# A softmax-convolution and cosine-FFN kernel: every product in two halves of 64 rows

## The chip, the core and the metric

The kernel runs on one core of a Trainium2 chip. The metric is the device time of one execution in microseconds (us). The engines are named as in the profile: PE (TensorE matmuls), PEld (TensorE weight loads), DVE (VectorE), ACT (ScalarE), POOL (GpSimd) and SP (SyncE, which issues the DMAs).

## The reference

Inputs are `x` (8 x 4096 x 192), `weight_gen` (8 x 4096 x 8 x 7), `w_in` (192 x 2048) and `w_out` (2048 x 192); the first two are float32, the weights float64.

```python
w = softmax(weight_gen, axis=-1)                        # 7 taps for each of 8 heads
a[b, s, h, :] = sum_k w[b, s, h, k] * x_padded[b, s + k, h, :]   # causal, 24 channels a head
h = a.reshape(32768, 192) @ w_in                        # 32768 x 2048
out = (h * cos(h)) @ w_out                              # 32768 x 192
```

## The kernel before, in words

**Tiling.** The 32768 tokens lie over 128 partitions, 256 in a row on each. A block is 4 tokens of every partition, 512 in all, and there are 64 blocks. POOL mixes the taps of a block into `xa` (lines 225 to 245). For each of the 4 tokens PE transposes `xa` in two pieces (line 257), channels 0 to 127 and the last 64 channels twice, so that both reach 128 rows. ACT and DVE split the transposed rows, divided by 2 pi, into two float32r parts whose sum is nearly exact: `a_hi`, `a_lo` for 128 channels and `b_hi`, `b_lo` for the 64 doubled ones (lines 264 and 265).

**First product** (line 282). A pair is two chunks of 128 of the 2048 columns of `w_in`; a block has 8 pairs and the program 512. A pair writes one tile `h` of 128 x 1024 (two PSUM banks) from a ring of three. Each chunk takes 5 matmuls of 512 columns: three for the 128 channels (low x high, high x low, high x high), two for the 64 channels, where `wb` holds the high part of the weights in rows 0 to 63 and the low part in rows 64 to 127 and the rows of `b` are there twice.

**Elementwise work** of pair i, on the 128 x 1024 of `h`: ACT rounds to `turn` (line 292), DVE subtracts (296), ACT takes the sine (300), DVE multiplies into `h` (303), ACT makes the high part `ghi` (309), DVE the low part `glo` in bf16 (313). Lines 309 and 313 are issued one pair later. The tile `h` is free after line 313.

**Second product.** A half of a block's chunks (8) is contracted at once for each token: 8 matmuls of 384 columns with `ghi` as weights (line 329) and 8 of 192 columns with `glo` (line 332), into a tile `ps_m` of one bank out of two. ACT copies it out (335) and POOL adds the two halves of the block and the two parts of the columns (346, 347). This follows the first product by 6 pairs (`LAG`), one group of 16 matmuls for each pair.

**Order.** Each engine issues in the order of the program, which is written out by the main loop: for pair i the first product, at pairs 5 and 6 of a block one of the two transposes (four matmuls) of the next block, the elementwise work of i, and then the second product of i - 6. The softmax of 16 rows (4 blocks) is done a step a pair, in 15 batches inside the loop: DVE maximum (179), POOL difference (181), ACT exponential (184), DVE sum (188, 189) and reciprocal (191), POOL product (193). The exponential and the next sine each load a table on ACT. While the first blocks run, the float64 words of the weights are converted on ACT, DVE and POOL (lines 112 to 132).

Of the kernel before, what the change touches and what calls it, by code (L numbers as in the profile page):

```python
# [20 lines left out]
P = 128  # L21
# [10 lines left out]
# sin(SIN_SCALE * f + SIN_BIAS) = cos(2 pi f) for -3/4 <= f <= 1/4; both constants are a few ulp  # L32
# below 2 pi and pi / 2, so that the argument stays within the table's [-pi, pi].
# [3 lines left out]
# The upper word of 2.0 ** -127 in float64, read as a float32: smaller values become denormal.  # L37
# [4 lines left out]
def tile_softmax_conv_then_cos_ffn(  # L42
# [58 lines left out]
    def two_parts(raw, hi, lo, half=None):  # L101
# [19 lines left out]
        # sign, exponent and 20 bits of the mantissa  # L121
# [3 lines left out]
        # 3 more bits of the mantissa  # L125
# [12 lines left out]

    def w_in_b(j):
        raw = words(CW)  # L140
        cols = [slice(n * (F // 2) + j * CW, n * (F // 2) + (j + 1) * CW) for n in range(2)]
        for n in range(2):
            nc.sync.dma_start(out=raw[n * D2:(n + 1) * D2], in_=w_in[P:D, cols[n]].bitcast(I32))

        def convert():
            parts = gpool.tile([P, 2, CW], F32R, name="parts", tag="ghi")
            yield from two_parts(raw, parts[:, 0, :], parts[:, 1, :])
            for n in range(2):
                for m in range(2):
# [64 lines left out]
    def attention(b, eng, ra=0, rb=R, spare=False):  # L214
# [3 lines left out]
        # the columns from D on repeat the last D2, for both halves of the transposed rows  # L218
# [14 lines left out]
        for k in range(1, K + 1):  # L233
            if k < K:
                if spare:
                    pr = work.tile([P, R, D], F32, name="pr", tag="turn", bufs=TMP)
                else:
                    pr = work.tile([P, R, D], F32, name="pr", bufs=3)
                product(k, pr[:, ra:rb])
                yield  # L240
# [10 lines left out]
    xT = {}  # L251

    def transposed(b, part):
        xa = mixed[b]
        tr = ps_m.tile([P, CT], F32, name="ps_m")
        for r in range(R):
            nc.tensor.transpose(  # L257
                tr[:, r * P:(r + 1) * P], xa[:, r, (0, P)[part]:(P, P + 2 * D2)[part]], ident)
        hi = work.tile([P, CT], F32R, name="ab"[part] + "_hi")
        lo = work.tile([P, CT], F32R, name="ab"[part] + "_lo")  # L260
        xT.setdefault(b, []).extend((hi, lo))

        def split():
            nc.scalar.activation(out=hi, in_=tr, func=AF.Copy, scale=1.0 / TWO_PI)
            nc.vector.scalar_tensor_tensor(  # L265
                out=lo, in0=tr, scalar=1.0 / TWO_PI, in1=hi.bitcast(F32),
                op0=ALU.mult, op1=ALU.subtract)

        return split

# [1 line left out]
    hs, g_parts = {}, {}  # L272

    def ffn_in(i):
        b, pair = divmod(i, NPAIR)
        a_hi, a_lo, b_hi, b_lo = xT[b]
        h = ps_h.tile([P, 2, CT], F32, name="h")
        for n in range(2):
            fs = slice((2 * pair + n) * P, (2 * pair + n + 1) * P)
            prods = ((wa_hi, a_lo), (wa_lo, a_hi), (wb, b_lo), (wb, b_hi), (wa_hi, a_hi))  # L280
            for m, (w, v) in enumerate(prods):
                nc.tensor.matmul(h[:, n, :], lhsT=w[:, fs], rhs=v,  # L282
                                 start=(m == 0), stop=(m == len(prods) - 1))
        hs[i] = h

# [30 lines left out]
    sums, finals = {}, {}  # L316

    def ffn_out(j):
        b, m = divmod(j, 2 * R)
        half, t = divmod(m, R)  # L320
        acc = ps_m.tile([P, CT], F32, name="ps_m")
        ts = slice(t * P, (t + 1) * P)
        for m in range(2):
            for c in range(2 * HALF):
                pair, n = divmod(c, 2)
                g = g_parts[b * NPAIR + half * HALF + pair][m][:, n, ts]
                fc = half * 2 * HALF + c
                if m == 0:
                    nc.tensor.matmul(acc[:, 0:2 * D], lhsT=g, rhs=wo[:, fc, :],  # L329
                                     start=(c == 0), stop=False)  # L330
                else:
                    nc.tensor.matmul(acc[:, 0:D], lhsT=g, rhs=wo_b[:, fc, :],  # L332
                                     start=False, stop=(c == 2 * HALF - 1))
        part = work.tile([P, 2 * D], F32, name=f"part{half}", bufs=(5 if half == 0 else 2))
        nc.scalar.activation(out=part, in_=acc[:, 0:2 * D], func=AF.Copy, scale=TWO_PI)  # L335
        if half == 0:
            sums[(b, t)] = part
            return
        if t == 0:
# [3 lines left out]
        old = sums.pop((b, t))  # L343
        last = b == NB - 1
        eng = nc.vector if last else nc.gpsimd
        eng.tensor_tensor(out=part, in0=part, in1=old, op=ALU.add)  # L346
        eng.tensor_tensor(out=fin[:, t, :], in0=part[:, 0:D], in1=part[:, D:2 * D], op=ALU.add)
        if t == R - 1 or (last and t == R - 2):
            t0 = t if last and t == R - 1 else 0
# [73 lines left out]
    for split in splits:  # L423
        split()
# [89 lines left out]
```

## Time and profile before

| | |
|---|---|
| runs | 2419.05 us median of 3 (2418.82 to 2419.44) |
| profiled execution: span from first to last instruction | 2416.5 us |
| PE busy | 2345.7 us |
| PEld busy | 2019.7 us |
| DVE busy | 2037.1 us |
| ACT busy | 1848.9 us |
| POOL busy | 1877.6 us |
| mean granted TensorE clock | 0.992 |

The profiled execution is one run of the program; its span is 2.55 us under the median of the runs. Matmuls are pipelined: the time that one takes in the rows (about 0.4 us) holds its way through the array, and what it costs in a stream is the distance between the starts of two. A weight load has a row of its own on PEld and lies beside the matmul before it.

### The profile page before, as it was taken

To read this page: it belongs to the slowest core of one execution; us is meant where nothing else is said; L and a number is where in the kernel's file an instruction comes from. 1 tells how busy PE (TensorE), PEld (TensorE's weight loads), DVE (VectorE), ACT (ScalarE), POOL (GpSimd) and SP (SyncE) were. 2 spreads that over 40 slices of the span, in tenths; PEclk is the share of its full clock that TensorE was granted. 3 is DMA by queue.
4 is the path that set the end of the run, shared out by engine and by line. 5 is a ranking of instruction groups with operands and counts; after the bars stand their busy time and mean duration, and the time that the engine had idled before them with its cause. 6 is when DMAs were issued, how large, how long until landed. Compare 5 with 4: busy or idle time off the path is not lost.

```text
span 2416.5 us, 34582 instructions
## 1 busy us (share of the span) xinstructions
PE 2345.7 (97%) x13824; PEld 2019.7 (84%) x13824; DVE 2037.1 (84%) x1820; ACT 1848.9 (77%) x2266; POOL 1877.6 (78%) x1458
## 2 busy tenths in 40 slices
PE   2799999999999999999999999999999999999999
PEld 1588888888888888888888888888888888888888
DVE  8988888888888888888888888888888888888887
ACT  3678777787877778777787777878777787777876
POOL 6698878797787787787787787877877877887841
PEclk8899999999999999999999999999999999999999
DMA  6211220210211120121211211111111201201100
GB/s 163 53 42 36 47 54 24 54 47 23 54 47 31 46 54 24 47 51 27 54 37 33 54 35 43 47 27 51 46 31 47 54 24 46 54 24 48 30 7 20
DMA packets 25456, 104.93 MB, mean 43 GB/s; under 512 B 2782, under 2 KB 5462, under 8 KB 25294
## 3 DMA queue, kind: packets, MB, share of 16 engines
q1 hardware_dynamic: 25294, 102.72, 17.1%
q8 instruction: 108, 1.77, 0.3%
q14 instruction: 54, 0.44, 0.1%
HBM read 76.50 MB, written 25.17 MB: 42 GB/s over the span
## 4 chain that ended last, share of the span: by engine, by line
PE 87%; DVE 6%; ACT 5%; issue 1%; DMA 0%; SPq 0%; ACTq 0%; DVEq 0%
PE h L282 46%; PE ps_m L329 27%; PE ps_m L332 13%; PE ps_m L257 2%; ACT ghi L309 1%; ACT turn L292 1%; DVE h L303 1%; DVE glo L313 1%; DVE den L189 1%; ACT L300 1%; DVE turn L296 1%; ACT turn L300 1%; DVE t L114 1%; ACT L184 1%; DVE den L188 1%
## 5 line engine op out<-in xcount | busy, mean ns | idle before, releaser
L296 DVE TENSOR_TENSOR turn<-h,turn 128x1024 f32<-128x1024 f32 x512 | 625.5, 1222 | 326.3 <-ACT turn L292 323.3
L329 PE MATMUL ps_m<-wo,ghi 128*128 128x384 f32 x4096 | 812.9, 340 | 3.1 <-ACT part L335 3.1
L292 ACT ACTIVATE turn<-h 128x1024 int32<-128x1024 f32 x512 | 524.7, 1025 | 314.3 <-PE h L282 314.3
L329 PEld LDWEIGHTS ps_m<-wo,ghi 128*128 128x128 f32 x4096 | 721.1, 188 | 38.3 <-ACT part L335 3.6
L245 POOL TENSOR_TENSOR xa<-xa,pr 128x768 f32<-128x768 f32 (+1 forms) x384 | 705.4, 1837 | 5.0
L300 ACT ACTIVATE turn<-turn 128x1024 f32<-128x1024 f32 x512 | 543.4, 1061 | 184.2 <-DVE turn L296 184.0
L303 DVE TENSOR_TENSOR h<-h,turn 128x1024 f32<-128x1024 f32 x512 | 629.9, 1230 | 8.3 <-ACT turn L300 8.3
L313 DVE TENSOR_TENSOR glo<-h,ghi 128x1024 bf16<-128x1024 f32 x512 | 621.7, 1214 | 1.1 <-ACT ghi L309 1.1
L225 POOL TENSOR_TENSOR pr<-xt,taps 128x768 f32<-128x768 f32 (+1 forms) x384 | 588.2, 1537 | 0.0
L346 POOL TENSOR_TENSOR part<-part,part 128x384 f32<-128x384 f32 x252 | 256.3, 1017 | 391.2 <-ACT part L335 391.1
L309 ACT CAST ghi<-h 128x1024 fp32r<-128x1024 f32 x512 | 516.3, 1008 | 3.8 <-DVE h L303 2.8
L282 PE MATMUL h<-a_lo,wa_hi 128*128 128x512 f32 x1024 | 454.3, 444 | 33.2 <-DVE glo L313 25.5
L332 PE MATMUL ps_m<-wo_b,glo 128*128 128x192 bf16 x4096 | 426.8, 247 | 0.0
L282 PE MATMUL h<-a_hi,wa_hi 128*128 128x512 f32 x1024 | 408.0, 398 | 0.0
L282 PE MATMUL h<-a_hi,wa_lo 128*128 128x512 f32 x1024 | 406.8, 397 | 1.1 <-POOL wa_lo L132 1.1
L282 PE MATMUL h<-b_hi,wb 128*128 128x512 f32 x1024 | 404.6, 395 | 0.0
L282 PE MATMUL h<-b_lo,wb 128*128 128x512 f32 x1024 | 403.6, 394 | 0.8 <-DVE b_lo L265 0.8
L332 PEld LDWEIGHTS <-glo 128*128 128x128 bf16 x4096 | 311.7, 98 | 82.1 <-issue 82.1
L282 PEld LDWEIGHTS h<-a_lo,wa_hi 128*128 128x128 f32 x1024 | 194.7, 190 | 62.6 <-ACT wa_hi L128 13.6
L335 ACT ACTIVATE part<-ps_m 128x384 f32<-128x384 f32 x512 | 241.4, 472 | 6.8 <-PE ps_m L332 6.8
L282 PEld LDWEIGHTS h<-b_lo,wb 128*128 128x128 f32 x1024 | 194.2, 190 | 48.9 <-DVE b_lo L265 1.3
L282 PEld LDWEIGHTS h<-b_hi,wb 128*128 128x128 f32 x1024 | 194.2, 190 | 45.5
(52 smaller groups left out, 1285.6 us busy)
## 6 DMA issues: line engine op xcount, KB each, us to landing
xt<-in_x_dram SPq DMA_DIRECT2D x62, 960.0 KB, 7.4
out_dram<-fin SPq DMA_DIRECT2D x63, 384.0 KB, 3.9
taps<-in_weight_gen_dram SPq DMA_DIRECT2D x15, 448.0 KB, 8.6
raw<-in_moe_w_out_dram SPq DMA_DIRECT2D x8, 384.0 KB, 3.9
raw<-in_moe_w_in_dram SPq DMA_DIRECT2D x6, 256.0 KB, 6.6
raw<-in_moe_w_in_dram SPq DMA_DIRECT2D x3, 512.0 KB, 5.9
wb<-parts SPq DMA_DIRECT2D x8, 128.0 KB, 4.8
xt<-in_x_dram SPq DMA_DIRECT2D x1, 768.0 KB, 11.7
```

The costliest lines, as they stand in the source:

```text
L225: eng.tensor_tensor(out=dst.rearrange("p r (h g) -> p r h g", h=H), in0=xt[:, k + ra:k + rb, :].rearrange("p r (h g) -> p r h g", h=H), in ...
L245: eng.tensor_tensor(out=xa[:, ra:rb, 0:D], in0=xa[:, ra:rb, 0:D], in1=old[:, ra:rb], op=ALU.add)
L282: nc.tensor.matmul(h[:, n, :], lhsT=w[:, fs], rhs=v, start=(m == 0), stop=(m == len(prods) - 1))
L292: nc.scalar.activation(out=t.bitcast(I32), in_=hs[i], func=AF.Identity, bias=0.25, scale=1.0)
L296: nc.vector.tensor_tensor(out=t, in0=hs[i], in1=t.bitcast(I32), op=ALU.subtract)
L300: nc.scalar.activation(out=t, in_=t, func=AF.Sin, bias=SIN_BIAS, scale=SIN_SCALE)
L303: nc.vector.tensor_tensor(out=hs[i], in0=hs[i], in1=turns.pop(i), op=ALU.mult)
L309: nc.scalar.copy(out=hi, in_=hs[i])
L313: nc.vector.tensor_tensor(out=lo, in0=hs.pop(i), in1=hi.bitcast(F32), op=ALU.subtract)
L329: nc.tensor.matmul(acc[:, 0:2 * D], lhsT=g, rhs=wo[:, fc, :], start=(c == 0), stop=False)
L332: nc.tensor.matmul(acc[:, 0:D], lhsT=g, rhs=wo_b[:, fc, :], start=False, stop=(c == 2 * HALF - 1))
L346: eng.tensor_tensor(out=part, in0=part, in1=old, op=ALU.add)
```

## The change

**Halves.** The array is used as two tiles of 64 rows, rows 0 to 63 and rows 64 to 127, which take their weights and their moving data from the same partitions. A product over 128 rows becomes two matmuls, one for each half, written one behind the other in the program. The two write different PSUM banks at one time. Since both halves of a sum belong in the same bank, they trade: in a first part the lower half writes bank 0 and the upper half bank 1, in a second part it is the other way round. Between the parts stands `traded`, a no-operation on SP that reads the tile: PE starts the second part when SP has passed, and SP passes when the first part has landed.

**First product.** A pair has 3 matmuls of each half in the first part (`ffn_in_first`) and 6 in the second (`ffn_in_second`). The 64 channels take 3 products over 64 rows (low x high, high x low, high x high): the two halves hold them for the two chunks. `wb` becomes `wb_hi` and `wb_lo`, loaded with the chunks of odd number in the upper rows, without the copies by DMA. The 6 pairs before the second product begins use whole products for the 128 channels and halves for the 64 (`ffn_in_whole`).

**Second product.** A group is two tokens and one half of the chunks. It takes two pairs (s = 0 and 1), each with 16 matmuls of 384 and 16 of 192 columns over 64 rows, into a tile `acc` of two banks, of which there is one. One ACT copy of 128 x 768 takes it out after the second pair, and POOL adds on 768 columns. The last 6 pairs use whole products.

**Order in the loop.** A pair i issues on PE the first part of h(i), the second product of i - 6, and the second part of h(i). The elementwise work of pair i comes in the next turn of the loop.

**Transposes.** For blocks 7 to 63 the transposes are four matmuls of 64 columns for each token, two in each pair, written to columns 384 to 511 of the two banks of `acc` between the `ghi` and the `glo` matmuls. ACT and DVE split them (`x_hi`, `x_lo`, 128 x 2 x 128) behind the copy of `acc`. Blocks 1 to 6 (`WHOLE`) are transposed whole, at pair 5, into a tile of the ring `h`.

**The rest.** The store of a block is issued three pairs later, the rows of the next block are loaded in the middle of a block's mixing, and `pr` has two buffers where it had three.

```diff
-    ps_m = ctx.enter_context(tc.tile_pool(name="ps_m", bufs=2, space=bass.MemoryType.PSUM))
+    ps_m = ctx.enter_context(tc.tile_pool(name="ps_m", bufs=1, space=bass.MemoryType.PSUM))
...
+    def traded(t):
+        nc.sync.keepalive_nop([nc.sync.lower_ap(t)])
...
+    def split(b, tr, cs):
+        hi, lo = parts_of(b)
+        nc.scalar.activation(out=hi[:, :, cs], in_=tr, func=AF.Copy, scale=1.0 / TWO_PI)
+        yield
+        nc.vector.scalar_tensor_tensor(
+            out=lo[:, :, cs], in0=tr, scalar=1.0 / TWO_PI, in1=hi[:, :, cs].bitcast(F32),
+            op0=ALU.mult, op1=ALU.subtract)
...
+    def transpose_all(b):
+        xa = mixed[b]
+        tr = ps_h.tile([P, 2, CT], F32, name="h")
...
+    def transpose_row(b, r, acc, s):
+        xa = mixed[b]
+        for q in range(2):
+            rs = slice(q * D2, (q + 1) * D2)
+            nc.tensor.matmul(acc[:, q ^ s, 2 * D + q * D2:2 * D + (q + 1) * D2],
+                             lhsT=xa[rs, r, columns(q ^ s)], rhs=ident[rs, rs], is_transpose=True,
...
+    def ffn_in_first(i):
+        h = ps_h.tile([P, 2, CT], F32, name="h")
+        for m, (w, v) in enumerate(((wa_hi, x_lo), (wa_lo, x_hi), (wa_hi, x_hi))):
+            for q in range(2):
+                rs = slice(q * D2, (q + 1) * D2)
+                nc.tensor.matmul(
+                    h[:, q, :], lhsT=w[rs, chunk(pair, q)], rhs=v[rs, 0, :],
...
+        traded(h)
...
+    def ffn_in_second(i):
+        prods = ((wa_hi, x_lo, 0), (wa_lo, x_hi, 0), (wb_hi, x_lo, 1), (wb_lo, x_hi, 1),
+                 (wa_hi, x_hi, 0), (wb_hi, x_hi, 1))
+        for m, (w, v, part) in enumerate(prods):
+            for q in range(2):
+                cs = chunk(pair, 1 - q) if part == 0 else slice(pair * P, (pair + 1) * P)
+                nc.tensor.matmul(
+                    h[:, 1 - q, :], lhsT=w[rs, cs], rhs=v[rs, part, :],
...
     def ffn_out(j):
+        if s == 0:
+            accs[group] = ps_m.tile([P, 2, CT], F32, name="acc")
...
+                for q in range(1 if whole else 2):
+                    rs = slice(0, P) if whole else slice(q * D2, (q + 1) * D2)
+                    bank = q ^ s
+                    t = 2 * tp + bank
+                    to, w = (acc[:, bank, 0:2 * D], wo) if lo == 0 else (acc[:, bank, 0:D], wo_b)
+                    nc.tensor.matmul(
+                        to, lhsT=g[rs, n, t * P:(t + 1) * P], rhs=w[rs, fc, :],
...
+            if lo == 0:
+                bt = group // R + 2
+                if WHOLE < bt < NB:
+                    transpose_row(bt, group % R, acc, s)
+        if s == 0 and not whole:
+            traded(acc)
...
+    def evacuate(j):
+        nc.scalar.activation(out=part, in_=acc[:, :, 0:2 * D], func=AF.Copy, scale=TWO_PI)
+        if WHOLE < bt < NB:
+            yield from split(bt, acc[:, :, 2 * D:], slice(r * P, (r + 1) * P))
...
-    for i in range(N + LAG):
+    for i in range(N + LAG + 1):
+        if 0 <= i - 1 < N:
+            act_turns(i - 1)
+        if 0 <= i - 2 < N:
+            act_hi(i - 2)
...
+            dve_fraction(i - 1)
+            act_cos(i - 1)
...
+            dve_lo(i - 2)
...
+            dve_g(i - 1)
...
+            if i < N:
+                ffn_in_first(i)
+            ffn_out(j)
+            if i < N:
+                ffn_in_second(i)
+        if pair == TR and b + 1 <= WHOLE:
+            until_mixed(b + 1)
+            tr = (transpose_all(b + 1),)
...
+            all_of(evacuate(j), *tr)
```

How the order moves on PE is shown for one pair in the middle of the program, from the first product of a pair to the first `glo` product. Before, the second chunk of a pair (`h`) is followed by the group of the second product (`ps_m`):

```order
L282 MATMUL h<-a_lo,wa_hi 128x512
L282 MATMUL h<-a_hi,wa_lo 128x512
L282 MATMUL h<-b_lo,wb 128x512
L282 MATMUL h<-b_hi,wb 128x512
L282 MATMUL h<-a_hi,wa_hi 128x512
L329 MATMUL ps_m<-wo,ghi 128x384 x8
L332 LDWEIGHTS glo
L332 MATMUL ps_m<-wo_b,glo 128x192
```

After the change the same engine issues the second part of one pair (line 343), the first part of the next (326), the `ghi` products (400) and two transposes (290); "x2" and "x16" are the two halves in turn:

```order
L343 MATMUL h<-x_lo,wa_hi 128x512 x2
L343 MATMUL h<-x_hi,wa_lo 128x512 x2
L343 MATMUL h<-x_lo,wb_hi 128x512 x2
L343 MATMUL h<-x_hi,wb_lo 128x512 x2
L343 MATMUL h<-x_hi,wa_hi 128x512 x2
L343 MATMUL h<-x_hi,wb_hi 128x512 x2
L326 MATMUL h<-x_lo,wa_hi 128x512 x2
L326 MATMUL h<-x_hi,wa_lo 128x512 x2
L326 MATMUL h<-x_hi,wa_hi 128x512 x2
L400 MATMUL acc<-wo,ghi 128x384 x16
L290 MATMUL acc<-ident,xa 128x64 x2
```

What moved: the tile `h` of a pair is now begun ahead of the second product and finished behind it, and the transposes stand inside the second product of every pair.

On DVE, in the middle of the program, at pairs 5 and 6 before the change (line 296 is the subtraction, 313 `glo`, 303 `h` times the cosine, 265 the split of the transposed rows):

```order
L296 TENSOR_TENSOR turn<-h,turn 128x1024
L265 SCALAR_TENSOR_TENSOR a_lo<-ps_m,a_hi 128x512
L313 TENSOR_TENSOR glo<-h,ghi 128x1024
L303 TENSOR_TENSOR h<-h,turn 128x1024
L296 TENSOR_TENSOR turn<-h,turn 128x1024
L265 SCALAR_TENSOR_TENSOR b_lo<-ps_m,b_hi 128x512
L313 TENSOR_TENSOR glo<-h,ghi 128x1024
```

After it, in every second pair (the same operations are lines 357, 374 and 364, and 272 is the split, which reads `acc`):

```order
L357 TENSOR_TENSOR turn<-h,turn 128x1024
L374 TENSOR_TENSOR glo<-h,ghi 128x1024
L364 TENSOR_TENSOR h<-h,turn 128x1024
L272 SCALAR_TENSOR_TENSOR x_lo<-acc,x_hi 128x2x128
L357 TENSOR_TENSOR turn<-h,turn 128x1024
```

What moved: the split stands behind the product of line 364, comes in every second pair, and is the last reader of the only `acc`.

More of the change, by code (lines that the diff above doesn't have):

```diff
@@ L248, in attention @@
             old = pr
-    xT = {}
-    def transposed(b, part):
-        xa = mixed[b]
[L255 to L269, printed above, removed]
+    xT, transposed = {}, set()
@@ new lines, in traded, with columns, parts_of @@
+    def traded(t):
+        nc.sync.keepalive_nop([nc.sync.lower_ap(t)])
+    def columns(part):
+        return slice(0, P) if part == 0 else slice(P, P + 2 * D2)
+    def parts_of(b):
+        if b not in xT:
+            hi = work.tile([P, 2, CT], F32R, name="x_hi")
+            lo = work.tile([P, 2, CT], F32R, name="x_lo")
+            xT[b] = (hi, lo)
+        return xT[b]
+    def split(b, tr, cs):
[5 more added lines that the diff above has]
+            op0=ALU.mult, op1=ALU.subtract)
@@ L313, in dve_lo @@
         nc.vector.tensor_tensor(out=lo, in0=hs.pop(i), in1=hi.bitcast(F32), op=ALU.subtract)
-    sums, finals = {}, {}
+    sums, finals, accs, stores = {}, {}, {}, {}
+    LATE = 3
     def ffn_out(j):
         b, m = divmod(j, 2 * R)
[L320 to L323, printed above, removed]
+        half, m = divmod(m, R)
+        tp, s = divmod(m, 2)
+        group = j // 2
+        if s == 0:
+            accs[group] = ps_m.tile([P, 2, CT], F32, name="acc")
+        acc = accs[group]
+        whole = j + LAG >= N
+        for lo in range(2):
@@ L324, in ffn_out @@
             for c in range(2 * HALF):
                 pair, n = divmod(c, 2)
-                g = g_parts[b * NPAIR + half * HALF + pair][m][:, n, ts]
+                g = g_parts[b * NPAIR + half * HALF + pair][lo]
                 fc = half * 2 * HALF + c
[L328 to L333, printed above, removed]
@@ L334, in ffn_out @@
-        part = work.tile([P, 2 * D], F32, name=f"part{half}", bufs=(5 if half == 0 else 2))
-        nc.scalar.activation(out=part, in_=acc[:, 0:2 * D], func=AF.Copy, scale=TWO_PI)
+                for q in range(1 if whole else 2):
[5 more added lines that the diff above has]
+                        to, lhsT=g[rs, n, t * P:(t + 1) * P], rhs=w[rs, fc, :],
+                        start=(lo == 0 and c == 0 and (whole or s == 0)),
+                        stop=(lo == 1 and c == 2 * HALF - 1 and (whole or s == 1)),
+                        skip_group_check=True)
@@ L418, in tile_softmax_conv_then_cos_ffn @@
     all_of(mix, attention(0, nc.vector, 0, 3))
-    splits = [transposed(0, part) for part in range(2)]
+    first = transpose_all(0)
     next(sm2)
@@ L422, in tile_softmax_conv_then_cos_ffn @@
     all_of(sm1)
-    for split in splits:
-        split()
+    all_of(first)
     next(sm2)
@@ L469, in tile_softmax_conv_then_cos_ffn @@
             next(sm, None)
-        for _ in range(2 if i else 4):
-            if (b if pair <= TR + 1 else b + 1) + 3 not in mixing:
-                next(bg, None)
+        for _ in range(4 if i == 0 else 2 + i % 2 if i < 60 else 2):
+            next(bg, None)
     issued = {}
```

157 lines of the change are left out of this document (96 added, 61 removed).

## The prediction

> **What bounds the kernel now.** I read the page first, then busy time by stretch, then the timeline of one pair on each engine.
>
> ```profile
> PE 2345.7 (97%) x13824; PEld 2019.7 (84%) x13824; DVE 2037.1 (84%) x1820; ACT 1848.9 (77%) x2266; POOL 1877.6 (78%) x1458
> PE 87%; DVE 6%; ACT 5%; issue 1%; DMA 0%; SPq 0%; ACTq 0%; DVEq 0%
> 400.00:1000.00 600.00, 597.89 (x3552) 516.49 (x3550) 506.87 (x444) 469.48 (x571) 477.87 (x369) 1.00 0.17 41
> ```
>
> PE holds 87% of the chain that ended last, and in 600 us of the middle it is idle for 2.1 at a granted clock of 1.00. The other engines wait for it. A shorter PE is worth its whole length until DVE or ACT, or the tiles that they hand back, come late. So I need PE's cost for each pair and the path of a tile through ACT and DVE. PE, one pair from its second product to the next:
>
> ```profile
> 1201.19 1.57 PE L329 MATMUL ps_m<-wo,ghi 128*128 128x384 f32 x8
> 1202.60 0.83 PE L332 MATMUL ps_m<-wo_b,glo 128*128 128x192 bf16 x8
> 1203.21 0.48 PE L282 MATMUL h<-a_lo,wa_hi 128*128 128x512 f32 x1
> 1203.53 0.39 PE L282 MATMUL h<-a_hi,wa_lo 128*128 128x512 f32 x1
> ...
> 1205.39 0.40 PE L282 MATMUL h<-a_hi,wa_hi 128*128 128x512 f32 x1
> 1205.62 0.69 PE L329 MATMUL ps_m<-wo,ghi 128*128 128x384 f32 x3
> ```
>
> From second product to second product are 4.43 us. From 1203.53 to 1205.39 are eight starts, 0.2325 us for a matmul of 512 columns. Ten of them are 2.325, so 2.10 are the second product with the changes of operand around it. A pair with transposes:
>
> ```profile
> 1216.51 0.48 PE L282 MATMUL h<-a_lo,wa_hi 128*128 128x512 f32 x1
> ...
> 1218.92 0.60 PE L257 MATMUL ps_m<-ident,xa 128*128 128x128 f32 x4
> ...
> 1221.37 0.48 PE L282 MATMUL h<-a_lo,wa_hi 128*128 128x512 f32 x1
> ```
>
> It lasts 4.86, so four transposes cost 0.43, or 0.107 each. A block is 8 x 4.43 + 0.86 = 36.30 us.
>
> **Part 1, the first product.** Two halves side by side take one slot of 0.2325 for what was one whole matmul. A pair then has 3 slots before the second product (0.70) and 6 behind it (1.395), 9 in place of 10. That removes 0.2325 x 512 = 119.0 us. The second product has 16 slots as before, 2.10.
>
> No row of before shows two halves at work at once. The loads decide whether it holds, since there are twice as many:
>
> ```profile
> L329 PEld LDWEIGHTS ps_m<-wo,ghi 128*128 128x128 f32 x4096 | 721.1, 188 | 38.3 <-ACT part L335 3.6
> L332 PEld LDWEIGHTS <-glo 128*128 128x128 bf16 x4096 | 311.7, 98 | 82.1 <-issue 82.1
> L257 PEld LDWEIGHTS ps_m<-ident,xa 128*128 128x128 f32 x512 | 64.6, 142 | 45.3 <-issue 27.7 <-DVE a_lo L265 0.8
> ```
>
> A load lies beside the matmul before it now. If the halves load side by side, a slot stays 0.2325; if their loads queue and a half takes as long as the whole, a pair needs 34 x 0.188 + 16 x 0.098 + 2 x 0.142 = 8.24 us of loading. I take side by side, because each half has rows of its own and the load of 188 ns already runs under another matmul's stream; the other end is a rival below. [...]
>
> **Part 2, transposes.** 57 blocks (7 to 63) lose 0.86, 49.0 us. In each pair two matmuls of 64 columns come in. Side by side by columns they cost half of 0.107, 0.054; by their load of 128 columns 0.107; one behind the other 0.215. I take 0.08 between the first two, T below: 57 x 8 x 0.08 = 36.5. Net -12.5.
>
> **Part 3, one `acc` and a longer path.** The ACT and DVE rows of one pair, the last matmul of its first product, and the split of before:
>
> ```profile
> 1196.52 0.40 PE L282 MATMUL h<-a_hi,wa_hi 128*128 128x512 f32 x1
> 1197.01 1.03 ACT L292 ACTIVATE turn<-h 128x1024 int32<-128x1024 f32 x1 [0.68 <-PE h L282]
> 1198.07 1.23 DVE L296 TENSOR_TENSOR turn<-h,turn 128x1024 f32<-128x1024 f32 x1 [0.85 <-ACT turn L292]
> 1199.21 1.22 DVE L313 TENSOR_TENSOR glo<-h,ghi 128x1024 bf16<-128x1024 f32 x1
> 1199.33 1.06 ACT L300 ACTIVATE turn<-turn 128x1024 f32<-128x1024 f32 x1 [0.39 <-DVE turn L296]
> 1200.43 1.23 DVE L303 TENSOR_TENSOR h<-h,turn 128x1024 f32<-128x1024 f32 x1
> L265 DVE SCALAR_TENSOR_TENSOR a_lo<-ps_m,a_hi 128x512 fp32r<-128x512 f32 x64 | 44.2, 691 | 12.0 <-ACT a_hi L264 12.0
> ```
>
> Count from S, the end of a pair's last slot (1196.52 + 0.23 = 1196.75). ACT rounds at +0.26, the subtraction starts 1.06 later (+1.32), the sine 1.26 later (+2.58), the product 1.10 later (+3.68). Behind it on DVE stands the split that frees `acc`: it starts 1.14 later (the distance of 1198.07 and 1199.21), takes 0.43 (691 ns for 512 columns, 1222 for 1024 of line 296, so 425 for 256), and with 0.06 of signal `acc` is free at +5.31. ACT's copy and `x_hi` are done by about +4.65 and don't decide. PE wants `acc` after first part, second product, second part and first part: 0.70 + 2.10 + T + 1.395 + 0.70 = 4.90 + T. It waits 0.41 - T = 0.33 in every second pair, four times a block, in 57 blocks: +75 us. Two pairs thus take 2 x (4.43 - 0.2325 + 0.08) + 0.33 = 8.89, a block 35.5 against 36.30.
>
> The ring of `h` gets tighter too. `glo` of pair k stands behind the subtraction of k + 1, so a tile is free at S(k+1) + 0.26 + 1.06 + 1.14 + 1.22 + 0.06 = 3.74; PE wants it for k + 3 one pair after S(k+1), at 4.28 or 4.61. Slack is 0.54 or 0.87. Before, a tile was begun only behind the second product, at 2.10 + 4.43 = 6.53, with 2.8 of slack. In that slack the softmax is hidden now:
>
> ```profile
> L184 ACT ACT_TABLE_LOAD x15 | 19.2, 1283 | 0.3
> L184 ACT ACTIVATE taps<-taps 128x896 f32<-128x896 f32 x15 | 14.3, 955 | 0.3
> L300 ACT ACT_TABLE_LOAD x15 | 19.2, 1283 | 0.3
> L188 DVE TENSOR_REDUCE den<-taps 128x128 f32<-128x896 f32 x15 | 16.1, 1076 | 0.0
> L189 DVE TENSOR_SCALAR den<-den 128x128 f32<-128x128 f32 x15 | 19.9, 1327 | 0.5
> PE h L282 <- DVE glo L313: 7.8, 11, 0.7
> ```
>
> From 400 to 2200 us PE waited 11 times, 0.7 a batch. After the change table and exponential put the rounding of pair 5 back by 2.2 us; less 0.87 of slack PE waits 1.3 for `glo` of pair 4. Behind that come the second table (1.3) and the sum's two operations on DVE (2.4). Of 5.9 in all, 1.3 are waited already, 0.87 is slack, and DVE's own gaps take up about 1.4 (4.44 a pair less 3.6 of work, over two pairs): 2.3 more, and 0.6 at the next `acc`. That is 4.2 a batch, 3.5 more than now, times 15: +52.
>
> **Part 4, blocks 1 to 6.** Their transposes take a tile of the ring at pair 5, and both splits of 1024 columns stand ahead of the elementwise work of pair 5. `glo` of pair 4 is then ready 0.86 + 0.26 + 1.07 + 1.14 (`x_hi`, `x_lo`) + 1.14 (subtraction) + 1.22 + 0.06 = 5.75 after S(5), with PE ready at 0.86: 4.9. Pair 7 gets the tile of pair 5, one turn sooner than else, and waits the 3.74. That is 8.6 a block. The first of the six falls where PE waits for the conversion of the weights already:
>
> ```profile
> PE h L282 <- DVE glo L313: 17.0, 5, 6.8
> ```
>
> That is up to 120 us, so I count five: +43.
>
> **Part 5, edits that I cost at nothing.** The no-operations on SP pass on a signal that PE needs one second product (2.10) or one second and first part (2.10) later; a DMA ahead of one on SP holds it for 0.86.
>
> ```profile
> 1191.28 0.86 SPq L173 DMA_DIRECT2D taps<-in_weight_gen_dram  x1
> ```
>
> Their cover is those 2.10; a DMA that waits for POOL would use it up, but POOL has 22% of idle time and the load in the middle of a block's mixing waits for a tile last read by the mixing before it. POOL's additions lie in that idle time. The copies of `wb` that go lie in the first 50 us beside other work.
>
> **Sum.** 2416.5 - 119.0 - 12.5 + 75 + 52 + 43 = 2455 for the span, and 2458 with the 2.55 us by which the median stands above this execution.
>
> **Rivals.** First, faster: the hand-overs are shorter than laid out. Where nothing else stood in the way I see distances below 1.14 on DVE:
>
> ```profile
> 1237.95 1.16 DVE L296 TENSOR_TENSOR turn<-h,turn 128x1024 f32<-128x1024 f32 x1
> 1239.02 1.21 DVE L313 TENSOR_TENSOR glo<-h,ghi 128x1024 bf16<-128x1024 f32 x1
> ```
>
> That is 1.07. Four steps lie ahead of the split; with 0.1 less in each the wait for `acc` is gone (-75) and the softmax costs 1 us less a batch (-15): 2458 - 90 = 2368. It decides from about 0.045 a step, where 0.18 x 228 = 41 brings the sum to no change. Against it: the rows of an undisturbed pair repeat to 0.01 us. If besides the halves stream at the rate of the bf16 rows (0.83 us for eight of 192 columns, 0.083 a start, 0.222 for 512), 9 slots are 0.09 shorter, of which the wait for `acc` takes about half: -25.
>
> Second, much slower: the loads of the halves queue. PE then needs 8.24 us in each of 506 pairs, with 92 us outside them (2416.5 less 512 x 4.54) 4260 us. For it speaks that PEld is at 84% with half the loads; against it, that each half has its own rows.
>
> **How the numbers follow.** My forecast, 0.60. Its own range: T from 0.054 to 0.215 gives -6 to +31, 0.05 in a step of the path 60 either way, so 2395 to 2525; 0.06 of the 0.60 lie within 0.2% of 2419, about what a measurement of this kernel can tell from no change, and 0.03 below. Faster rival 0.30, from 2343 to 2395. Queued loads 0.10. So faster 0.33, same 0.06, slower 0.61. The range 2345 to 2530 leaves out the queued loads and some 0.08 of the edges.
>
> **What would show it.** Right: matmuls of 64 rows in twos at one start, slots of 0.23; PE idle ahead of line 400 on DVE line 272, about 0.3 us 230 times; PE idle ahead of line 326 on DVE line 374, some 4 us a softmax batch and 8 to 9 in each of blocks 0 to 5; busy time of PE near 2215 (2345.7 less 119.0 and 12.5). Wrong: starts of halves 0.19 apart with PEld full; or PE waiting for SP or POOL; or `acc` free before PE asks.

## The result, and the profile after

| | before | after |
|---|---|---|
| runs | 2419.05 us | 2449.12 us median of 4 (2447.49 to 2449.39) |
| ratio | | 1.0124, 95% interval 1.0109 to 1.0138 |
| span of the profiled execution | 2416.5 us | 2447.6 us |
| mean granted TensorE clock | 0.992 | 0.985 |

The kernel became slower by 30 us, where 39 were forecast. The page of the changed kernel, busy time and the chain that ended last:

```profile
PE 2278.4 (93%) x26436; PEld 1951.2 (80%) x26436; DVE 2034.2 (83%) x1923; ACT 1833.8 (75%) x2117; POOL 1848.4 (76%) x1206
PE 53%; DVE 25%; ACT 12%; issue 9%; DMA 1%; ACTq 0%; SPq 0%; DVEq 0%
```

PE's share of the chain fell from 87% to 53%, and DVE and ACT together hold 37%: PE has less to do and now waits for them. The same 600 us of the middle as before, by stretch (PE, PEld, DVE, ACT, POOL, then the granted clock):

```profile
400.00:1000.00 600.00, 576.05 (x6804) 494.82 (x6800) 502.68 (x476) 464.04 (x537) 471.80 (x303) 1.00 0.18 43
```

PE is idle for 24.0 us instead of 2.1. PE's timeline of a pair without a wait:

```profile
1201.21 0.48 PE L343 MATMUL h<-x_lo,wa_hi 64*128 64x512 f32 x2
...
1202.93 0.39 PE L326 MATMUL h<-x_hi,wa_lo 64*128 64x512 f32 x2
1203.16 0.39 PE L326 MATMUL h<-x_hi,wa_hi 64*128 64x512 f32 x2
1203.38 1.57 PE L400 MATMUL acc<-wo,ghi 64*128 64x384 f32 x16
1204.79 0.22 PE L290 MATMUL acc<-ident,xa 64*128 64x64 f32 x2
1204.85 0.82 PE L400 MATMUL acc<-wo_b,glo 64*128 64x192 bf16 x16
1205.45 0.48 PE L343 MATMUL h<-x_lo,wa_hi 64*128 64x512 f32 x2
```

Two matmuls of 64 rows stand at one start ("x2", 0.003 us apart in the trace), and the next two start 0.23 later. The second product takes 1.41 and 0.60 as before. The pair lasts 4.24 us, with its two transposes in 0.06, against 4.43 without any. This pair in every place would have been a gain. The waits of PE:

```profile
PE acc L400 <- DVE x_lo L272: 47.2, 228, 0.5
PE h L326 <- DVE glo L374: 42.6, 31, 3.9
...
PE h L326 <- DVE x_lo L272: 14.2, 6, 2.4
```

Three of them matter here: for `acc` in every second pair of the 57 blocks, for a tile of the ring `h`, most of it around the softmax batches, and for the split of a block that is transposed whole. No wait of PE for SP or POOL is among those of the middle. Next, the hand-over of `acc` on all engines, one pair behind the one above:

```profile
1204.01 1.22 DVE L357 TENSOR_TENSOR turn<-h,turn 128x1024 f32<-128x1024 f32 x1 [1.09 <-ACT turn L353]
1205.15 1.21 DVE L374 TENSOR_TENSOR glo<-h,ghi 128x1024 bf16<-128x1024 f32 x1
...
1206.36 1.23 DVE L364 TENSOR_TENSOR h<-h,turn 128x1024 f32<-128x1024 f32 x1
...
1207.40 0.40 PE L326 MATMUL h<-x_hi,wa_hi 64*128 64x512 f32 x2
1207.50 0.41 DVE L272 SCALAR_TENSOR_TENSOR x_lo<-acc,x_hi 128x256 fp32r<-128x256 f32 x1
1207.97 1.68 PE L400 MATMUL acc<-wo,ghi 64*128 64x384 f32 x16 [0.17 <-DVE x_lo L272]
...
1209.48 0.22 PE L290 MATMUL acc<-ident,xa 64*128 64x64 f32 x2
```

The split `x_lo` stands on DVE behind the subtraction, `glo` and the product, and PE starts its second product 0.06 after the split ends. PE's start is 0.57 behind the last matmul of the first part, 0.34 more than a slot of 0.2325. The bracket says 0.17 only, because the row of that matmul is 0.40 long, 0.17 more than a slot, and covers the rest. And the `ghi` products then take 1.51 (1207.97 to 1209.48) where they took 1.41: the load of their first weights starts late too (at 1207.97, with the first product; in the pair above at 1203.16, 0.22 ahead of it). One such hand-over costs 0.34 + 0.10 = 0.44.

PE around one softmax batch, and around the transposes of block 2:

```profile
515.11 0.50 PE L326 MATMUL h<-x_lo,wa_hi 64*128 64x512 f32 x2 [1.13 <-DVE glo L374]
...
521.02 0.50 PE L326 MATMUL h<-x_lo,wa_hi 64*128 64x512 f32 x2 [1.40 <-DVE glo L374]
...
522.48 2.93 PE L400 MATMUL acc<-wo,ghi 64*128 64x384 f32 x16 [0.49 <-DVE x_lo L272]
```

```profile
131.69 0.42 PE L343 MATMUL h<-x_hi,wb_hi 64*128 64x512 f32 x2
132.04 1.10 PE L281 MATMUL h<-ident,xa 128*128 128x128 f32 x8
135.51 0.50 PE L326 MATMUL h<-x_lo,wa_hi 64*128 64x512 f32 x2 [2.37 <-DVE x_lo L272]
...
136.31 2.50 PE L400 MATMUL acc<-wo,ghi 64*128 64x384 f32 x16
138.61 1.51 PE L400 MATMUL acc<-wo_b,glo 64*128 64x192 bf16 x16
139.82 0.58 PE L343 MATMUL h<-x_lo,wa_hi 64*128 64x512 f32 x2
```

In both places the second product behind the wait is slow without waiting: 2.50 and 1.51 for the two groups instead of 1.57 and 0.82. The stretches of those two say why, in the sixth figure behind the length (the first line is the stretch ahead of the first of them):

```profile
133.20:136.62 3.42, 1.11 (x10) 0.98 (x12) 2.39 (x3) 2.82 (x4) 3.34 (x4) 1.00 0.00 0
136.62:140.03 3.41, 3.41 (x34) 3.06 (x32) 2.32 (x2) 1.05 (x1) 3.33 (x3) 0.50 0.00 0
...
522.32:525.73 3.41, 3.25 (x24) 3.14 (x26) 3.41 (x5) 2.36 (x3) 2.30 (x2) 0.50 0.01 2
```

The granted clock is 0.50 in both, and 1.00 ahead of them.

### The profile page after: what moved, and what is told of

It reads as the page before. It is cut to its first block, busy times and chain, and to the rows that moved or that the text cites. A ratio compares the mean times of both kernels' runs of the same rounds, so it can differ in the third digit from the quotient of the medians.

```text
span 2447.6 us, 60709 instructions
## 1 busy us (share of the span) xinstructions
PE 2278.4 (93%) x26436; PEld 1951.2 (80%) x26436; DVE 2034.2 (83%) x1923; ACT 1833.8 (75%) x2117; POOL 1848.4 (76%) x1206
## 4 chain that ended last, share of the span: by engine, by line
PE 53%; DVE 25%; ACT 12%; issue 9%; DMA 1%; ACTq 0%; SPq 0%; DVEq 0%
PE acc L400 30%; PE h L343 19%; DVE turn L357 9%; DVE glo L374 8%; ACT turn L353 7%; DVE x_lo L272 4%; PE h L326 4%; DVE h L364 1%; ACT x_hi L270 1%; ACT L183 1%; ACT turn L361 1%; ACT ghi L370 1%; PE acc L290 1%; DVE den L187 1%; DMA taps<-in_weight_gen_dram 1%
## 5 line engine op out<-in xcount | busy, mean ns | idle before, releaser
L400 PE MATMUL acc<-wo,ghi 64*128 64x384 f32 x8144 | 838.5, 343 | 50.1 <-DVE x_lo L272 47.2
L400 PEld LDWEIGHTS acc<-wo,ghi 64*128 64x128 f32 x8144 | 723.6, 187 | 173.4 <-DVE x_lo L272 145.9
L437 POOL TENSOR_TENSOR part<-part,part 128x768 f32<-128x768 f32 x126 | 232.2, 1843 | 483.4 <-ACT part L421 483.3
L400 PE MATMUL acc<-wo_b,glo 64*128 64x192 bf16 x8144 | 424.3, 243 | 0.0
L400 PEld LDWEIGHTS <-glo 64*128 64x128 bf16 x8144 | 331.4, 94 | 25.4 <-issue 7.8
L326 PE MATMUL h<-x_lo,wa_hi 64*128 64x512 f32 x1012 | 206.4, 402 | 56.9 <-DVE glo L374 42.6
L343 PE MATMUL h<-x_lo,wa_hi 64*128 64x512 f32 x1012 | 241.9, 473 | 0.0
L421 ACT ACTIVATE part<-acc 128x768 f32<-128x768 f32 x256 | 203.3, 794 | 9.2 <-PE acc L400 9.2
L343 PE MATMUL h<-x_lo,wb_hi 64*128 64x512 f32 x1012 | 202.4, 395 | 0.0
L326 PE MATMUL h<-x_hi,wa_hi 64*128 64x512 f32 x1012 | 201.6, 393 | 0.0
L343 PE MATMUL h<-x_hi,wa_hi 64*128 64x512 f32 x1012 | 201.1, 392 | 0.0
L326 PE MATMUL h<-x_hi,wa_lo 64*128 64x512 f32 x1012 | 200.7, 391 | 0.0
```

The lines of the kernel that those rows point to most:

```text
L326: nc.tensor.matmul(h[:, q, :], lhsT=w[rs, chunk(pair, q)], rhs=v[rs, 0, :], start=(m == 0), stop=False, skip_group_check=True)
L343: nc.tensor.matmul(h[:, 1 - q, :], lhsT=w[rs, cs], rhs=v[rs, part, :], start=False, stop=(m == len(prods) - 1), skip_group_check=True)
L400: nc.tensor.matmul(to, lhsT=g[rs, n, t * P:(t + 1) * P], rhs=w[rs, fc, :], start=(lo == 0 and c == 0 and (whole or s == 0)), stop=(lo == 1 ...
```

## The experiments

**What does the softmax cost, before and after?** The same edit in both kernels leaves the softmax of blocks 7 to 63 out; those blocks use the taps of blocks 3 to 6.

```diff
-            sm = softmax(r0, min(r0 + RW, RPP), nc.gpsimd)
+            for k in range(min(SB, NB - b - 4)):
+                taps[b + 4 + k] = taps[3 + k]
+                ready.add(b + 4 + k)
```

In the changed kernel:

> Leaves out the softmax of blocks 7 to 63 (they use the weights of blocks 3 to 6 again). Theory: the waits of 1.3 and 1.57 us at line 326 in each of 14 batches go, with what they cost at the next acc and in clock, so 45 to 55 us: 2399 us (2390 to 2410). Rival (the softmax is hidden as it was before the change): 2440 to 2449.

In the kernel before:

> The kernel before without the softmax of blocks 7 to 63 (they use the weights of blocks 3 to 6 again). Theory (its ring has 2.8 us of slack and hides the softmax): it gains the 8 to 10 us that PE waited, 2407 to 2413, so that of the 54 us which the softmax costs after the change 45 are new. Rival (the softmax costs both kernels the same): about 2365.

Measured: 2395.07 us after (ratio 0.99, 0.9883 to 0.9916) and 2407.02 before (0.9951, 0.9934 to 0.9967). The softmax thus costs 54 us after the change and 12 before, and 42 are new. In the first of the two the waits of line 326 for `glo` went, those for `acc` stayed:

```profile
PE acc L400 <- DVE x_lo L272: 44.1, 228, 0.4
...
PE h L326 <- DVE glo L374: 5.4, 2, 3.9
```

Without the softmax the changed kernel would be ahead of before in its present form by 24 us and of the same cut by 12, so two bounds of different size work here: one in the hand-over of `acc`, one in the ring.

**The hand-over, made longer.** The same `x_lo` is written twice:

```diff
             yield from split(bt, acc[:, :, 2 * D:], slice(r * P, (r + 1) * P))
+            hi, lo = parts_of(bt)
+            cs = slice(r * P, (r + 1) * P)
+            nc.vector.scalar_tensor_tensor(out=lo[:, :, cs], in0=acc[:, :, 2 * D:], ...)
```

> DVE makes x_lo of every riding transpose twice, both times from acc, so that acc comes free one such operation later (0.34 us from start to start). Theory (that path sets the wait for acc): 228 x 0.34 = 78 us more, up to 98 with the full 0.43: 2527 to 2547. Rival (DVE has slack, 17% idle, and the wait has another cause): 2449 to 2460.

Measured: 2572.27 us (1.0633, 1.0617 to 1.0649), 123 more than the changed kernel. PE's wait for `acc`:

```profile
PE acc L400 <- DVE x_lo L428: 171.4, 227, 1.1
```

All of it lies in that wait: 171.4 less 47.2 is 124 (the ring's waits fell by 8 beside it, from 42.6 to 34.7). So DVE's queue ahead of `acc` sets PE's time, and nothing takes up an operation that is added there. The size was above what was expected: the second `x_lo` starts 0.44 behind the first, 100 us in 228 places. Of the other 24 some 21 lie behind it: PE starts 0.15 after the second `x_lo` ends (1206.05 to 1206.20; 0.14 to 0.16 in every place that the rows show), where it was 0.06. Why that step became longer stays open.

**The hand-over, taken off DVE.** ACT copies the transposed columns to SBUF, and both parts are made from the copy, so that `acc` is free when ACT is done:

```diff
-            yield from split(bt, acc[:, :, 2 * D:], slice(r * P, (r + 1) * P))
...
+            xs = work.tile([P, 2, P], F32, name="xs")
+            nc.scalar.activation(out=xs, in_=acc[:, :, 2 * D:], func=AF.Copy, scale=1.0 / TWO_PI)
+            nc.scalar.copy(out=hi[:, :, cs], in_=xs)
+            yield
+            nc.vector.tensor_tensor(out=lo[:, :, cs], in0=xs, in1=hi[:, :, cs].bitcast(F32), op=ALU.subtract)
```

> The transposed columns of acc are copied out by ACT (divided by 2 pi) behind its copy of the sums, and x_hi and x_lo are made from that copy, so that DVE's split no longer holds acc. Theory (the only acc is handed back late because DVE's split stands behind its product): ACT is done about 4.70 us after the end of a pair's last slot and PE asks at 4.94, so the wait ahead of line 400 goes, 228 times 0.34 us and the 0.10 by which the loads behind a wait start late, about 100 us; the ring of h loses the slack that the wait gave and takes some 5 to 10 us back in the softmax batches. 2355 us (2335 to 2375). Rival (the elementwise path as a whole is the bound and the wait only moves to the ring of h, line 326 on glo): 2420 to 2450.

Measured: 2432.06 us (1.0053, 1.0038 to 1.0068 against before), better than the change by 17 and far from what was expected. PE's wait for `x_lo` ahead of `acc` is gone, but PE waits more often for the ring:

```profile
PE h L326 <- DVE glo L374: 76.2, 107, 3.9
```

DVE's part of the split in this kernel, and in the changed one, where one of its operands is in PSUM (busy us, then mean ns of one):

```profile
L431 DVE TENSOR_TENSOR x_lo<-xs,x_hi 128x256 fp32r<-128x256 f32 x228 | 342.8, 1504 | 49.0 <-ACT x_hi L429 49.0
```

```profile
L272 DVE SCALAR_TENSOR_TENSOR x_lo<-acc,x_hi 128x256 fp32r<-128x256 f32 x228 | 95.0, 417 | 0.0
```

It takes 1504 ns where it took 417. One of them and POOL's addition beside it, from the timelines of DVE and of POOL:

```profile
976.46 1.47 DVE L431 TENSOR_TENSOR x_lo<-xs,x_hi 128x256 fp32r<-128x256 f32 x1 [0.18 <-ACT x_hi L429]
```

```profile
975.79 1.86 POOL L443 TENSOR_TENSOR part<-part,part 128x768 f32<-128x768 f32 x1 [3.27 <-ACT part L421]
```

It ends at 977.93, 0.28 behind the end of POOL's addition (977.65), as if it had waited for that. Sixteen of the 228 fell where POOL was idle, the one below between POOL's instructions that ended at 958.61 and began at 960.51:

```profile
959.08 0.42 DVE L431 TENSOR_TENSOR x_lo<-xs,x_hi 128x256 fp32r<-128x256 f32 x1 [0.18 <-ACT x_hi L429]
```

All sixteen took 0.42 or 0.43, as from PSUM; each of the other 212 ended 0.27 to 0.30 behind the end of the instruction that POOL was at. So it is POOL's work that holds this subtraction up, and not the two operands in SBUF alone.

**The same, with the low part on POOL.** One word of the last edit: `nc.gpsimd.tensor_tensor` makes `x_lo`.

> As the run in which ACT copies the transposed columns out, but POOL makes x_lo in place of DVE. Theory (there DVE's x_lo from two SBUF operands took 1.47 us in place of 0.42 and put all behind it back): without it on DVE the ring waits outside the softmax go, and acc stays free in time: 2355 us (2340 to 2380). Rival (POOL, 76% busy, is late with xa or with x_lo for the next block): over 2400, with PE waiting for POOL at line 290 or at the first part.

Measured: 2368.95 us (0.9795, 0.978 to 0.9809), ahead of both kernels. What `x_lo` takes on POOL, and the wait of PE that is left in the loop:

```profile
L431 POOL TENSOR_TENSOR x_lo<-xs,x_hi 128x256 fp32r<-128x256 f32 x228 | 168.6, 740 | 218.7 <-ACT x_hi L429 218.7
```

```profile
PE h L326 <- DVE glo L374: 54.8, 31, 3.9
```

POOL has the 169 us to spare, and nobody on PE's side asks for `acc` before ACT's copies are done.
Against the changed kernel this is 80 us. The hand-over was 0.44 x 228 = 100, and 12 of it came back in the ring (54.8 less 42.6). The mean granted clock of 0.982, where the changed kernel has 0.985, makes some 7 us over the span, about the 8 that are still missing.

**The split ahead of the product.** Another way to free `acc` early: `x_hi` before the copy of `acc` on ACT, and `x_lo` before the product on DVE.

```diff
-        part = work.tile([P, 2, 2 * D], F32, name=f"part{half}", bufs=2)
-        nc.scalar.activation(out=part, in_=acc[:, :, 0:2 * D], func=AF.Copy, scale=TWO_PI)
...
             yield from split(bt, acc[:, :, 2 * D:], slice(r * P, (r + 1) * P))
+        product()
+        part = work.tile([P, 2, 2 * D], F32, name=f"part{half}", bufs=2)
+        nc.scalar.activation(out=part, in_=acc[:, :, 0:2 * D], func=AF.Copy, scale=TWO_PI)
...
-        if 0 <= i - 1 < N:
-            dve_g(i - 1)
+        def product(i=i):
+            if 0 <= i - 1 < N:
+                dve_g(i - 1)
```

> Same instructions as the change, in another order behind every second pair: x_hi on ACT ahead of the copy of the sums, and x_lo on DVE ahead of the product h times cosine. Theory (acc is late because the split stands behind that product on DVE): acc is then free at about 4.71 us after the end of a pair's last slot, by ACT's copy, against 4.94 at which PE asks; the product comes 0.6 later, and behind it on DVE stands the next subtraction, which waits for PE anyway. The wait ahead of line 400 goes, some 100 us, and some 10 come back in the ring: 2357 us (2340 to 2375), under the kernel before. Rival (the wait moves to the ring, as most of it did when x_lo was made from SBUF): 2420 to 2445.

Measured: 2500.74 us (1.0338, 1.0323 to 1.0353), slower than the change and above both expectations. The timeline of ACT, DVE and PE:

```profile
1006.30 0.42 DVE L272 SCALAR_TENSOR_TENSOR x_lo<-acc,x_hi 128x256 fp32r<-128x256 f32 x1 [0.27 <-ACT x_hi L270]
...
1006.82 0.81 ACT L427 ACTIVATE part<-acc 128x768 f32<-128x768 f32 x1 [0.55 <-DVE x_lo L272]
...
1007.69 1.68 PE L400 MATMUL acc<-wo,ghi 64*128 64x384 f32 x16 [0.21 <-ACT part L427]
```

DVE is done early, as meant. But ACT's copy of the other columns of the same banks starts only behind `x_lo` (0.10 us after its end, with 0.55 of idle time ahead): in this program ACT and DVE read a bank one behind the other. The copy of 0.81 became the last step, and ACT's next rounding stands behind it. PE's wait for `acc` went from 47.2 to 90.8 us and the ring's from 42.6 to 50.1, together about the 52 us by which this run is behind the change.

**Only the 64 channels in halves.** Into the kernel before, nothing but the three products over 64 channels, with `wb_hi` and `wb_lo` loaded as in the change:

```diff
+        for m, (w, v) in enumerate(((wb_hi, b_lo), (wb_lo, b_hi), (wb_hi, b_hi))):
+            for q in range(2):
+                rs = slice(q * D2, (q + 1) * D2)
+                nc.tensor.matmul(h[:, 1 - q, :], lhsT=w[rs, pair * P:(pair + 1) * P],
+                                 rhs=v[rs, :], start=(m == 0), stop=False)
...
-            prods = ((wa_hi, a_lo), (wa_lo, a_hi), (wb, b_lo), (wb, b_hi), (wa_hi, a_hi))
...
+            for m, (w, v) in enumerate(((wa_hi, a_lo), (wa_lo, a_hi), (wa_hi, a_hi))):
```

> The kernel before, with one part of the change alone: the 64 channels as three products in two halves of 64 rows, 9 slots in place of 10, and everything else whole. Each pair then changes twice between whole and halved array. Theory (halves work side by side, a change costs time: one row after the change shows halves to whole 0.12 us longer than a slot): 512 x 0.2325 = 119 us less, 2 x 0.12 x 512 = 123 us more, about 2420 us (2380 to 2460), which is why every product had to be halved. Rival (a change of the mode costs nothing in a stream): 2300 us (2295 to 2310), as the ring has 2.8 us of slack there.

Measured: 2475.78 us (1.0234, 1.0219 to 1.0249). The pair has the 9 slots of the change and needs 4.56 us (1201.46 to 1206.02 by the starts of two second products), more than the 4.43 with 10. PE's timeline, halves between whole products:

```profile
1202.88 0.84 PE L332 MATMUL ps_m<-wo_b,glo 128*128 128x192 bf16 x8
1203.64 0.50 PE L278 MATMUL h<-b_lo,wb_hi 64*128 64x512 f32 x2
...
1204.21 0.39 PE L278 MATMUL h<-b_hi,wb_hi 64*128 64x512 f32 x2
1204.54 0.50 PE L283 MATMUL h<-a_lo,wa_hi 128*128 128x512 f32 x1
1204.87 0.39 PE L283 MATMUL h<-a_hi,wa_lo 128*128 128x512 f32 x1
```

To the halves are 0.76 instead of 0.61, and from them 0.33 twice instead of 0.2325. In all a pair is 0.13 longer although a slot went, so the two changes cost 0.13 + 0.2325 = 0.36, or 0.18 each. Twice 0.18 is more than the slot. That is why halves pay here only when every product is in halves, with the trading of banks and the one `acc` that this brings.

**All blocks transposed whole.** The changed kernel with one number changed:

```diff
-    WHOLE = 6
+    WHOLE = 63
```

> All blocks are transposed whole into a tile of the ring, none rides in acc. acc is then freed by ACT's copy: no wait ahead of line 400 (0.44 a second pair less), and 0.44 a block less on PE; each block has 0.86 of transposes, two changes between halves and whole (0.19 each) and a wait. Theory (pair 6 takes the tile that the transposes give back and waits 2.4 for x_lo, once): 2.2 less and 3.7 to 5.1 more for each of 57 blocks, 2535 to 2615. Rival (the ring turns in order, 4.9 and 3.7 of waits, as the prediction had it): about 2850.

Measured in one run: 2571.79 us, mean clock 0.966. There is one wait a block (149.4 us in 63 waits, the longest 2.4) and no second one for pair 7:

```profile
1219.44 0.50 PE L326 MATMUL h<-x_lo,wa_hi 64*128 64x512 f32 x2 [2.37 <-DVE x_lo L272]
...
1220.24 1.57 PE L400 MATMUL acc<-wo,ghi 64*128 64x384 f32 x16
```

PE waits for the split itself: it takes the place of `h` that the transposes give back, and doesn't go round the ring for another. Behind this wait the clock holds (1.57), behind the same one at 135.51 in the changed kernel it didn't; in this run it fell behind some 27 of the 63, and its mean is lower for that.

**The softmax's batch, eased.** With the low part on POOL, the ring's waits around the softmax are the largest left. First the addition of 1e-9 goes to POOL, and the batch begins a pair later (`SMP = 3`):

```diff
-        nc.vector.tensor_scalar_add(out=den, in0=den, scalar1=1e-9)
+        eng.tensor_scalar_add(out=den, in0=den, scalar1=1e-9)
...
-    SMP = 2
+    SMP = 3
```

> As the run in which POOL makes x_lo, with the softmax moved: it begins one pair later, so that the exponential with its two table loads falls on a pair in which ACT has no copies of acc (1.0 us less ahead of the rounding), and POOL adds the 1e-9 to the sum (1.33 us less on DVE). Theory (the ring of h has 0.5 us of slack, so what is put ahead of a pair's elementwise work is waited for nearly whole): of 2.1 and 2.6 us at line 326 in each of 14 batches some 2 go, and some of the slow clock behind them: 2339 us (2325 to 2355). Rival (the waits are set by the table loads and by POOL's share of the softmax alone): 2360 to 2372.

Measured: 2368.22 us (0.979, 0.9774 to 0.9807), the same as without. PE's waits between 400 and 2200 us:

```profile
PE h L326 <- DVE glo L374: 23.8, 12, 2.0
PE acc L400 <- ACT xs L428: 7.8, 12, 0.8
```

They come to 31.6 us, where 40.9 stand without the edit (the line is below), so PE did wait less, by 9. The granted clock took that back: its mean is 0.978 here and 0.982 without, which is 9 to 10 us over a span of 2366. In the rows of ACT the exponential was held up as well, by 0.89 us at 508.98, because POOL's difference was not done when ACT came to it. So the last edit moves the exponential without the difference, and leaves the addition on DVE:

```diff
             out=t, in0=t, in1=top.unsqueeze(2).broadcast_to([P, n, K]), op=ALU.subtract)
         yield
+        if r0 >= 3 * R + RW:
+            yield
```

> The kernel with the low part on POOL (2368.95 us), with one edit: the softmax's exponential, sum, reciprocal and product come one pair later, so that the exponential falls into the other kind of pair, the one behind which no copy of acc follows at once, and POOL's difference is done long before it. Theory A (where the exponential falls decides what its 3.5 us with two tables cost PE: with the copies of acc between the wait grows, without them it shrinks): 2345 us, 2335 to 2358, the waits of line 326 for glo about 25 us instead of 40.9 between 400 and 2200 us. Theory B (the ring's slack is the same in every pair, the batch costs PE the same 2.1 and 2.55 wherever it stands): 2365 to 2372.

Measured: 2355.79 us (0.9738, 0.9721 to 0.9754). The time lies in the range of the first theory, at its upper end. PE's waits between 400 and 2200 us, with the exponential where it was:

```profile
PE h L326 <- DVE glo L374: 40.9, 24, 2.4
```

and one pair later:

```profile
PE h L328 <- DVE glo L376: 22.5, 20, 1.3
PE acc L402 <- ACT xs L430: 10.5, 13, 0.8
```

Where it stood, ACT had the copy of `acc` and both steps of the split right ahead of it, and the next rounding came late by the sum of all. One pair later these lie apart: the waits are smaller, 33.0 in sum and none above 1.3 us. The copy that is gone from beside the exponential is the one right ahead of it, where the expectation spoke of the one that follows; no run tells the two apart. And the waits are not the whole of it: the run before this one waits as little (31.6) and takes 12.4 us longer. Its mean granted clock is 0.978 and this one's 0.983, which is 12 us over the span. So, by these figures, where the exponential falls decides PE's waits, and the clock behind them decided how much of that the time kept. This is the best version here, 2.6% ahead of before and 3.8% of the change.

**Both parts behind the second product.** With the low part on POOL, the first part of a pair is moved behind the second product, so that the tile of `h` is asked for later:

```diff
-            if i < N:
-                ffn_in_first(i)
             ffn_out(j)
             if i < N:
+                ffn_in_first(i)
                 ffn_in_second(i)
```

> As the run in which POOL makes x_lo, but both parts of the first product stand behind the second product, so that nothing covers the hand-over over SP between them, and the ring of h gets the 2.1 us of slack back. Theory (the hand-over takes some 0.4 to 0.5 us from the end of the last matmul, hidden so far): PE stands that long ahead of line 343 in each of 506 pairs, the next second product asks for acc earlier and waits a little, and the softmax waits go: 2369 + 230 to 290 - 40 to 80, about 2570 us (2520 to 2620), and each pair's gap can be read. Rival (SP passes the signal in no time): a gap under 0.1 us and about 2480 us or less.

Measured in one run: 2578.6 us. Now nothing lies between the two parts, and the trade of banks is on the path:

```profile
1203.55 0.40 PE L326 MATMUL h<-x_hi,wa_hi 64*128 64x512 f32 x2
1204.04 0.50 PE L343 MATMUL h<-x_lo,wa_hi 64*128 64x512 f32 x2
```

The two starts are 0.49 apart, 0.26 beyond a slot, and the next start comes 0.34 later (1204.38) where a slot is 0.2325. In 506 pairs that is 131 and 54 of the 210 us over the version with the parts apart. The other 25 were not taken apart, but behind the softmax PE now waits up to 4.2 us for `acc`, 57.2 us in 14 waits. So the time came as expected, though the trade itself, 0.37, is a little cheaper than was thought; the second product between the parts hides it.

## Why the prediction was right in its direction, step by step

| step | forecast, us | measured, us |
|---|---|---|
| Part 1, first product | -119.0 | slots of 0.2325: -119 |
| Part 2, transposes | -12.5 | -49 + 456 x 0.055 = -24 |
| Part 3, wait for `acc` | +75 | 0.44 x 228 = +100 |
| Part 3, softmax and ring | +52 | 54 - 12 = +42 |
| Part 4, whole transposes | +43 | 3 x 4.3 + 2 x 2.9 = +19 |
| last groups | - | +5 |
| sum of the span | +38.5 | +23 of 31.1 |

The sum came nearer than its terms. Part 2 was 11 too dear, the wait for `acc` 25 too cheap, the ring 10 and Part 4 24 too dear, and 13 us had no term at all. These took each other off in part: that the total came within 9 us is luck.

**Part 1 held.** No run of before shows two halves in one slot, as the -119.0 has them; that was the author's choice. After the change the halves do load and stream side by side: a load of a half takes 187 ns (a whole one took 188), yet slots are 0.23 with two loads in each, which start 0.003 us apart. The rival of the queued loads, 8.24 us a pair, fell: 1201.21 to 1205.45 is 4.24.

**Part 2** was in the right place, and the size is at the cheap end: two transposes stand 0.055 ahead of the `glo` products, by the side-by-side price of 0.054 and not the 0.08 taken.

**Part 3, the wait for `acc`, was right in mechanism, place and count** (228 times, from DVE's `x_lo`). The path was as counted: 1204.01 to 1205.15 is the 1.14, and with T at 0.055 the wait of 0.41 - T is 0.355 against 0.34 measured. What was left out is the late start of loading behind a wait, 0.10 each time, 23 us. The faster rival asked for steps of 1.07 in the loop, and these didn't come. That its sum of 2368 is the time of the version with the low part on POOL (2368.95) rests on the same price: that is about what the kernel takes when `acc` doesn't wait.

**Part 3, the ring.** The forecast has two steps of 1.3 and 2.3 with 0.6 at `acc`. The waits of the batch above are 1.13 and 1.40 by the brackets, and the second was less than thought. Four of the batches pay for the slow clock behind it, as with 2.93 instead of 1.57 at 522.48. The whole, 42, is near 52.

**Part 4 is the step that failed.** The forecast was that `glo` of pair 4 stands behind the splits (4.9 us) and that pair 7 then waits 3.7 more. PE waits for `x_lo` alone, once: 132.04 to 135.51 is 3.47, of which 0.86 are the transposes, 2.61. Added to that are 0.12 for the change from halves and 1.5 in the next second product at the slow clock (136.31 to 139.82 is 3.51 where 2.0 is usual). That makes 4.2, half of the forecast, and more than a third of it is a cost that the forecast didn't have. By the distances between second products, three of the five blocks pay 4.2 to 4.4 like this one, and two, behind which the clock held, 2.9: 19 us in all. The run with all blocks whole shows the single wait 63 times.

**Part 5 held**: no wait for SP or POOL is in the loop.

**The check on PE's busy time was wrong.** Near 2215 us was named, and the page says 2278.4. Busy time is no floor: it holds matmuls at the slow clock, and the ends of matmuls that hang over into a wait (a row of 0.40 us where a slot is 0.2325). In the 600 us PE shows 24.0 idle; yet a pair lasts 4.59 there on average (pairs 41 to 496, by the starts of their second products), so 131 fit in, their work is 131 x 4.24 = 555, and 45 were lost.

The last groups, which the forecast left out, take 26.04 us from the last second product in halves to the end (2421.56 to 2447.6), where before it was 19.74 from the same group (2396.76 to 2416.5). Of the 6.3 between them 1.4 is a second part that stands behind that product now; in the other 5 are two waits for ACT's copy of `acc`, 2.98. About 8 us of the 31 are not covered by the steps; 3.7 of them stand already when the first second product starts. Their cause wasn't tried.

## What to carry to other kernels

A faster product pays only as far as the engines behind it hand their tiles back; count the path from the last matmul of a tile to the next write of it, and expect each wait to cost more than its idle row (here 0.44 us where the row shows 0.17). When one buffer is what is left, put its release on the engine with the shortest queue ahead of it: here the same change, with the release on ACT, the rest of the split on POOL and the exponential one pair later, went from 1.2% slower to 2.6% faster. Move all products to a tiling or none, if a change between tilings costs about what a slot does (here 0.18 us against 0.2325).

## What the runs showed of the hardware

- A change between whole products and halves costs some 0.18 us in the kernel with only the 64 channels in halves (4.56 us a pair with 9 slots, 4.43 with 10 and no change), and 0.12 in the changed kernel, where the rows show one alone (131.69 to 132.04 less a slot).
- A wait of 0.34 us for `acc` in the changed kernel costs 0.10 more in the 16 products behind it (1.51 in place of 1.41).
- The granted clock of the changed kernel goes to half for stretches of 3.41 us, eight times between 105 and 2430 us. PE was busy for 17% to 52% of the 3.41 us ahead of each (1.11 of 3.42 at 133.20, 1.68 of 3.41 at 518.91); of the stretches that were followed by full clock the least busy had 50%, the next 53%. So in this run some half of a stretch of idle time was enough, in one piece or in two. The wait of 2.37 us at 135.51 falls into one stretch. In the run with all blocks whole the one at 1219.44 is divided by an edge at 1218.53 (1.95 of 3.41 us busy ahead of it, 2.51 of 3.42 behind it), and the clock held.
- With the low part made from SBUF on DVE, a subtraction of 256 columns with both operands in SBUF took 0.42 or 0.43 us where POOL was idle (16 of 228), and else ended 0.27 to 0.30 us behind the end of POOL's instruction, 1504 ns on average over the 228; with one operand in PSUM, in the changed kernel, it took 417 ns.
